# Routing attention and a hard-swish feed-forward block on one core: the first batch's second product in seven half products, and the weight sums in one row

## The chip, the cores and the metric

One core of a Trainium2 chip runs the whole program. The metric is the device time of one execution in microseconds (us). The engines are named as the profile names them: PE (TensorE matmul), PEld (its weight load), DVE (VectorE), ACT (ScalarE), POOL (GpSimd) and SP (SyncE, which issues the DMAs here).

## The reference

Four batches of 768 tokens go through an attention with 8 heads of 64, in which a query sees only the keys of its own cluster, and then through a feed-forward block with 512 inputs, 2048 hidden units and 512 outputs:

```
q_assign = argmax(q_n . c_n); k_assign = argmax(k_n . c_n)          # 16 clusters for each head
scores   = where(q_assign == k_assign, (q @ k^T) / 8, -1e9)
x        = softmax(scores) @ v                                      # (4, 8, 768, 64) -> (3072, 512)
h        = x @ w_in                                                 # (3072, 2048)
g        = h * clip(h + 3, 0, 6) / 6
out      = g @ w_out                                                # (3072, 512)
```

The inputs q, k, v and centroids are float32; the two weight matrices arrive as float64.

## The kernel before, in words

The program is one list of instructions in an order written out by hand, with no scheduler inside it. A loop runs over n = 0, 2, 4, ... and each turn of it, called "step n" here, handles attention units n and n+1. A unit is one block of 128 keys against half (384) of the queries, for a pair of heads. Twelve units make a pair of heads, 48 a batch, 192 all. A step emits, in this order:

- `scores` of units n and n+1 (L354 into the PSUM tile ps, then the exponential on ACT, L366, then an add into acc on POOL, L370 or L373, from the second unit of a half on);
- `attn_v` of the two units before (L383, into pv);
- every third step `divide` (pd by TensorE from the sum acc, L404; its reciprocal on VectorE, L408; and the product into xT, L409). It comes at steps 8, 14, 20 and so on, among them 56, 62, 68, 74, 80, 86, 92 and 98;
- preparation of the next pair: in the steps with n mod 12 equal to 0 and 2 two `turn`s each (pqk, L278, copied to xf by ACT, L280), at 4 `cluster_scores` (pcs, L291), at 6 `route` (pr by TensorE, L302, and then seven VectorE operations up to one_hot, L306 to L322), at 8 and 10 `route_turn` (po, L334);
- some feed-forward items from the list `fill`, alternating with the preparation (first an item, then a preparation part, and so on);
- in 32 chosen steps, the last of them step 94, `decode_weights`: one chunk of a weight matrix is turned from float64 into float32 by five VectorE operations (L217, L221, L224, L228, L231) and two on ACT (L208, L211). Its raw data were loaded by an SP DMA one decoding step earlier.

A batch's feed-forward items can begin when its last xT is there. The first batch's are added at step 50; the function `items_by(n)` says how many items must have been emitted by step n. DECODED is 96, the step after the last decode, and END is 104.

Two kinds of items exist before the change. `ffn_items`, for the first batch only, is the plain form: an up item is four matmuls of 384 columns into ph (L440), followed by the gate (ACT L427, VectorE L428); a down item is four matmuls of 512 columns into py (L457), and four of them make a row block of the output. For a half batch these are 16 ups and 12 downs. `fast_items`, for the other three batches, works on blocks of 256 tokens (m = 0, 1, 2). An up item is eight matmuls of 256 columns (L504), a gate 512 wide, and after every second one four VectorE sums of the gated blocks (L516, the S sums). Then seven down items, each one half product: eight matmuls of 256 columns (L522) into the banks X and Y, with five adds (L529 to L557) and two copies, in place of the eight half products of a plain 2x2 block product. In the profile every float32 matmul has two records, so that an up item of eight matmuls shows as 16.

Seven half products need sums of the weight blocks: `weight_sums(i)`, i = 0 to 7, makes T1, T2, T4 and T3 in halves, each one VectorE subtraction of 128x1024 (L493). T3 overwrites one quarter of w_out itself. Before the change the eight are emitted one a step, in steps 96 to 110, at the end of the step.

PSUM: ps has two double banks, pv one, and the rest is two pools: `psum_m` with two banks, which ph, py, X and Y take from, and `psum_t` with one. The helper `scratch` serves pqk, pcs, pr, po and pd; up to step 96 it takes two of three from psum_m and the third from psum_t, and from step 96 on (`st["early"] = False`) all from psum_t.

Of the kernel before, what the change touches and what calls it, by code (L numbers as in the profile page):

```python
# [8 lines left out]
F32 = mybir.dt.float32  # L9
# [9 lines left out]
P = 128  # L19
NCH = S // P  # L20
NC2 = 2 * NCH
HALF = S // 2
NHC = NCH // 2
# [93 lines left out]
def fast_path(ctx, tc, ok, q, k, v, centroids, moe_w_in, moe_w_out, out):  # L117
# [310 lines left out]
        nc.vector.scalar_tensor_tensor(out=g, in0=g, scalar=1.0, in1=h, op0=ALU.min, op1=ALU.mult)  # L428


    def ffn_items(b):
        slots = g_sb.rearrange("p k i c -> p (k i c)")

        def up(hf, f):
            def item():
                xT = st["xT", b]
                ph = psum_m.tile([P, 512], F32, name="ph", tag="m")
                hh = ph[:, 0:HALF]
                for kt in range(NKT):
                    nc.tensor.matmul(  # L440
                        hh, lhsT=w_in_sb[:, kt, f * P : (f + 1) * P],
                        rhs=xT[:, kt, hf * HALF : (hf + 1) * HALF],
                        start=(kt == 0), stop=(kt == NKT - 1),
                    )
                at = (hf * NFT + f) % 18 * HALF
                st["g", f] = slots[:, at : at + HALF]
                gate(st["g", f], hh)

            return item

        def down(hf, i, part):
            def item():
                if part == 0:
                    st["y"] = psum_m.tile([P, DM], F32, name="py", tag="m")
                py = st["y"]
                for f in range(part * 4, part * 4 + 4):
                    nc.tensor.matmul(  # L457
                        py, lhsT=st["g", f][:, i * P : (i + 1) * P], rhs=w_out_sb[:, f],
                        start=(f == 0), stop=(f == NFT - 1),
                    )  # L460
                if part == 3:
                    y = yp.tile([P, DM], F32, name="y", tag=f"y{i % 2}")
                    nc.vector.tensor_copy(out=y, in_=py)
                    nc.sync.dma_start(out_v[b, hf * NHC + i], y)

            return item

        items = []
        for hf in range(2):
            items += [up(hf, f) for f in range(NFT)]  # L470
            items += [down(hf, i, part) for i in range(NHC) for part in range(4)]
        return items

# [15 lines left out]
        nc.vector.tensor_tensor(out=st[name][:, h], in0=a[:, h], in1=b[:, h], op=ALU.subtract)  # L493


    def fast_items(b):
        def up(m, i):
            def item():
                xT = st["xT", b]
                ph = psum_m.tile([P, 512], F32, name="ph", tag="m")  # L500
                for t in range(2):
                    f = t * HF + i
                    for kt in range(NKT):
                        nc.tensor.matmul(  # L504
                            ph[:, t * HC : (t + 1) * HC], lhsT=w_in_sb[:, kt, f * P : (f + 1) * P],
                            rhs=xT[:, kt, 2 * m * P : 2 * (m + 1) * P],
                            start=(kt == 0), stop=(kt == NKT - 1),
                        )
                gate(g_sb[:, 0:4, i], ph.rearrange("p (k c) -> p k c", k=4))
                if i % 2:  # L510
                    a11, a21, a12, a22, s1, s2, s4 = (g_sb[:, k, i - 1 : i + 1] for k in range(7))
                    for out_, in0, in1, op in (
                        (s1, a21, a22, ALU.add), (s2, s1, a11, ALU.subtract),
                        (a21, a11, a21, ALU.subtract), (s4, a12, s2, ALU.subtract),
                    ):
                        nc.vector.tensor_tensor(out=out_, in0=in0, in1=in1, op=op)  # L516

            return item

        def product(bank, half, kind, w, first, last, again):  # L520
            for i in range(HF):
                nc.tensor.matmul(  # L522
                    bank[:, half * HC : (half + 1) * HC], lhsT=g_sb[:, kind, i], rhs=w[:, i],
                    start=(first and i == 0), stop=(last and i == HF - 1),
                    skip_group_check=again,
                )

        def add(out_, in0, in1):
            nc.vector.tensor_tensor(out=out_, in0=in0, in1=in1, op=ALU.add)  # L529

        def down(m, part):
            def item():
                if part == 0:
                    st["X"] = psum_m.tile([P, DM], F32, name="X", tag="m")
                    st["y0"] = yp.tile([P, DM], F32, name="y0", tag="y0")
                elif part == 2:
                    st["Y"] = psum_m.tile([P, DM], F32, name="Y", tag="m")
                    st["y1"] = yp.tile([P, DM], F32, name="y1", tag="y1")
                kind, bank, half, w = (
                    (0, "X", 0, wb[0][0]), (5, "X", 1, st["T2"]),  # L540
                    (4, "Y", 0, st["T1"]), (1, "Y", 1, st["T3"]),
                    (2, "X", 0, wb[1][0]), (6, "Y", 0, wb[1][1]), (3, "Y", 1, st["T4"]),
                )[part]
                product(st[bank], half, kind, w, part in (0, 2), part in (1, 3, 4, 6), part > 3)
                y0, y1 = st["y0"], st.get("y1")
                if part == 1:
                    nc.scalar.copy(out=y0[:, HC:], in_=st["X"][:, HC:])
                    add(y0[:, HC:], y0[:, HC:], st["X"][:, 0:HC])
                elif part == 3:
                    add(y1[:, 0:HC], y0[:, HC:], st["Y"][:, HC:])  # L550
                    add(y1[:, HC:], y1[:, 0:HC], st["Y"][:, 0:HC])
                elif part == 4:
                    nc.scalar.copy(out=y0[:, 0:HC], in_=st["X"][:, 0:HC])
                elif part == 6:
                    add(y1[:, 0:HC], y0[:, HC:], st["Y"][:, HC:])
                    nc.sync.dma_start(out_v[b, 2 * m + 1], y1)
                    add(y0[:, HC:], y0[:, HC:], st["Y"][:, 0:HC])  # L557
                    nc.sync.dma_start(out_v[b, 2 * m], y0)

            return item  # L560

        items = []
        for m in range(NHC):
            items += [up(m, i) for i in range(HF)] + [down(m, part) for part in range(7)]
        return items
# [20 lines left out]
    per_batch = NKT * per_pair  # L586
    total = NPAIR * per_pair
    lag_v, lag_d = 2, 4
    up_half = NFT
    per_ffn = 2 * (NFT + NHC * 4)  # L590
    per_fast = NHC * (HF + 7)

# [8 lines left out]
    def items_by(n):  # L603

        if n <= DECODED:
            return max(n - READY, 0) * up_half // (DECODED - READY)
        if n <= END:
            return up_half + (n - DECODED) * (per_ffn - up_half) // (END - DECODED)
        return per_ffn + (n - END) * per_fast // per_batch

    st["early"] = True
    fill, later = [], []
# [2 lines left out]
    with tc.manual_schedule():  # L615
# [16 lines left out]
        for n in range(0, total + lag_d + 2, 2):  # L632
            g, r = divmod(n, per_pair)
            for i in (n, n + 1):
                if i < total:
                    scores(i)
            for i in (n - lag_v, n - lag_v + 1):
                if 0 <= i < total:
                    attn_v(i)
            for check in later:  # L640
                check()
            later = []
            m = n - lag_d + 1
            if m >= 0 and m % NCH == NCH - 1:
                later.append(divide(m))
            prep = prep_items(g + 1, r)
            if r == 4 and prep:
                prep.pop()()
            if n == DECODED:
                st["early"] = False  # L650
            if m >= 0 and m % per_batch == per_batch - 1:
                fill += (fast_items if m >= per_batch else ffn_items)(m // per_batch)
            if r == 6:
                load(g + 2, "q", "k")
                load(g + 1, "v")
            want = items_by(n + 2) - done if n < total else len(fill)
            want = min(want, len(fill))
            done += want
            for i in range(max(len(prep), want)):
                if i < want:  # L660
                    fill.pop(0)()
                if i < len(prep):
                    prep[i]()
            if n in slots:
                load_weights(slots.index(n) + 1)
                decode_weights(slots.index(n))
            if n >= DECODED and (n - DECODED) // 2 < 8:
                weight_sums((n - DECODED) // 2)
            if n >= total:
                for check in later:  # L670
                    check()
                later = []
# [381 lines left out]
```

## Time and profile before

| | us |
|---|---|
| median of 10 runs | 1108.46 (1107.1 to 1109.28) |
| the profiled execution: its time | 1108.44 |
| the profiled execution: its span, first to last instruction | 1106.6 |
| PE, DVE, ACT, POOL busy in the span | 1049.0, 466.9, 384.8, 301.3 |
| mean granted PE clock | 0.983 of full speed |

Times in the profile count from the start of the span. A row of a group gives line, engine, operation, output<-inputs, count, busy time in us and the mean of one in ns. Rows of the chain give a start and a length in us, and follow the work that ended last back to what released it. Step 48 begins at 138.0 us (its first exponential), step 96 at 304.9, and the matmuls of step 104's up item at 447.0.

### The profile page before, as it was taken

The numbers are of one execution on the slowest core, as the hardware profiler recorded it, in microseconds if no ns is written. First come the engines' busy times: TensorE is split into PE (matmuls) and PEld (weight loads), VectorE is DVE, ScalarE is ACT, GpSimd is POOL, SyncE is SP. The second block draws the span as 40 slices with busy tenths as digits, with TensorE's granted clock in tenths as the row PEclk, the third lists the DMA queues.
The fourth block names the chain that finished last, engine by engine and source line by source line (L and its number), as shares of the span: only waits on it lengthen the run. The fifth ranks groups of instructions, "written<-read, shape, count | busy, mean of one in ns | idle before, by whom it ended". The sixth has DMA issues, their size and how long they took to land.

```text
span 1106.6 us, 12777 instructions
## 1 busy us (share of the span) xinstructions
PE 1049.0 (95%) x5218; PEld 674.6 (61%) x5218; DVE 466.9 (42%) x654; ACT 384.8 (35%) x734; POOL 301.3 (27%) x187
## 2 busy tenths in 40 slices
PE   5988888999799999999999999999999999999996
PEld 3433334444344544676676777667676678888885
DVE  6799996688612220342240332333133141413131
ACT  4666665666411310332333332332333230101010
POOL 3666653554401100323222232322323320000000
PEclk8999998999899999999999999999999999999999
DMA  5333341342202000020110202001100000000000
GB/s 130 90 93 88 94 119 58 101 119 70 69 10 59 3 1 20 10 43 1 33 30 1 63 1 44 20 12 32 34 1 1 20 1 1 20 4 16 20 1 24
DMA packets 83541, 42.90 MB, mean 39 GB/s; under 512 B 76304, under 2 KB 76304, under 8 KB 83472
## 3 DMA queue, kind: packets, MB, share of 16 engines
q1 hardware_dynamic: 83328, 41.95, 14.7%
q8 instruction: 43, 0.70, 0.3%
q14 instruction: 26, 0.21, 0.1%
q10 hardware_dynamic: 144, 0.03, 0.0%
HBM read 35.68 MB, written 6.29 MB: 38 GB/s over the span
## 4 chain that ended last, share of the span: by engine, by line
PE 81%; DVE 16%; issue 1%; ACT 1%; POOL 0%; DVEq 0%; POOLq 0%
PE ph L504 23%; PE Y L522 11%; PE ps L354 11%; PE X L522 9%; PE pv L383 8%; PE py L457 7%; PE ph L440 6%; DVE rcp L408 3%; DVE wtop L221 2%; DVE one_hot L322 2%; DVE wtop L217 2%; PE pqk L278 2%; DVE wunit L228 1%; DVE xT L409 1%; PE pd L404 1%
## 5 line engine op out<-in xcount | busy, mean ns | idle before, releaser
L373 POOL TENSOR_TENSOR acc<-acc,ex 128x768 f32<-128x768 f32 x128 | 239.1, 1868 | 405.5 <-ACT ex L366 400.0
L504 PE MATMUL ph<-xT,w_in_sb 128*128 128x256 f32 x1152 | 259.6, 382 | 0.0
L504 PEld LDWEIGHTS ph<-xT,w_in_sb 128*128 128x128 f32 x1152 | 215.3, 190 | 46.2 <-issue 18.1
L366 ACT ACTIVATE ex<-ps 128x768 f32<-128x768 f32 x192 | 151.0, 806 | 150.8 <-PE ps L354 149.7
L428 DVE SCALAR_TENSOR_TENSOR g_sb<-g_sb,ph 128x512 f32<-128x512 f32 (+1 forms) x104 | 67.1, 645 | 282.6 <-ACT g_sb L427 282.6
L354 PE MATMUL ps<-xf 64*128 64x384 f32 x768 | 172.8, 529 | 5.2 <-ACT ex L366 5.2
L427 ACT ACTIVATE g_sb<-ph,half_c 128x512 f32<-128x512 f32 (+1 forms) x104 | 68.1, 655 | 313.9 <-PE ph L504 249.6
L383 PE MATMUL pv<-ex,vt 128*64 128x384 f32 x768 | 146.4, 503 | 0.0
L370 POOL TENSOR_TENSOR acc<-ex 128x768 f32<-128x768 f32 x32 | 59.4, 1857 | 200.3 <-ACT ex L366 200.3
L408 DVE RECIPROCAL rcp<-pd 128x384 f32<-128x384 f32 x32 | 81.7, 2553 | 62.0 <-PE pd L404 62.0
L354 PEld LDWEIGHTS ps<-xf 64*128 64x128 f32 x768 | 65.8, 193 | 53.2 <-issue 34.6
L383 PEld LDWEIGHTS pv<-ex,vt 128*64 128x64 f32 x768 | 47.1, 138 | 82.9 <-issue 79.5
L440 PE MATMUL ph<-xT,w_in_sb 128*128 128x384 f32 x256 | 87.3, 493 | 2.0 <-DVE g_sb L428 2.0
L457 PE MATMUL py<-w_out_sb,g_sb 128*128 128x512 f32 x192 | 84.0, 594 | 0.0
L440 PEld LDWEIGHTS ph<-xT,w_in_sb 128*128 128x128 f32 x256 | 47.2, 190 | 41.5 <-issue 4.8
L529 DVE TENSOR_TENSOR y<-y,Y 128x256 f32<-128x256 f32 x36 | 15.1, 420 | 125.4 <-PE Y L522 124.8
L522 PE MATMUL Y<-w_out_sb,g_sb 128*128 128x256 f32 x288 | 66.1, 383 | 0.0
L354 PE MATMUL ps<-xm 64*128 64x384 bf16 x384 | 65.2, 334 | 0.7 <-ACT xm L338 0.7
L522 PE MATMUL Y<-T,g_sb 128*128 128x256 f32 x288 | 65.3, 380 | 0.0
L522 PE MATMUL X<-w_out_sb,g_sb 128*128 128x256 f32 x288 | 65.3, 380 | 0.0
L457 PEld LDWEIGHTS py<-w_out_sb,g_sb 128*128 128x128 f32 x192 | 35.9, 190 | 44.2 <-issue 43.0
L522 PEld LDWEIGHTS Y<-w_out_sb,g_sb 128*128 128x128 f32 x288 | 53.9, 190 | 12.9 <-issue 6.0
(88 smaller groups left out, 854.8 us busy)
## 6 DMA issues: line engine op xcount, KB each, us to landing
raw<-in_moe_w_in_dram SPq DMA_DIRECT2D x16, 512.0 KB, 3.6
raw<-in_moe_w_out_dram SPq DMA_DIRECT2D x16, 512.0 KB, 3.6
qk<-in_q_dram SPq DMA_DIRECT2D x32, 192.0 KB, 3.8
qk<-in_k_dram SPq DMA_DIRECT2D x32, 192.0 KB, 4.3
vt<-in_v_dram SPq DMA_DIRECT2D x32, 192.0 KB, 4.2
out_dram<-y SPq DMA_DIRECT2D x24, 256.0 KB, 2.1
cen<-in_centroids_dram ACTq DMA_DIRECT2D x1, 32.0 KB, 1.7
```

Source lines behind the costliest of these rows:

```text
L354: nc.tensor.matmul(st["ps", n][:, t, 0:HALF], lhsT=x[r, NCH + j], rhs=x[r, hf * NHC : (hf + 1) * NHC], start=first, stop=not first,)
L366: nc.scalar.activation(out=ex, in_=sc, func=ACT.Exp, scale=SM_SCALE)
L370: nc.gpsimd.tensor_tensor(out=acc, in0=st["ex", n - 1], in1=ex, op=ALU.add)
L373: nc.gpsimd.tensor_tensor(out=acc, in0=acc, in1=ex, op=ALU.add)
L383: nc.tensor.matmul(pv[t * D : (t + 1) * D], lhsT=vt[:, j, t], rhs=ex[:, t], start=(j == 0), stop=(j == NCH - 1),)
L408: nc.vector.reciprocal(out=rcp, in_=pd)
L427: nc.scalar.activation(out=g, in_=h, func=ACT.Relu, bias=half_c, scale=1.0 / 6.0)
L428: nc.vector.scalar_tensor_tensor(out=g, in0=g, scalar=1.0, in1=h, op0=ALU.min, op1=ALU.mult)
L440: nc.tensor.matmul(hh, lhsT=w_in_sb[:, kt, f * P : (f + 1) * P], rhs=xT[:, kt, hf * HALF : (hf + 1) * HALF], start=(kt == 0), stop=(kt == ...
L457: nc.tensor.matmul(py, lhsT=st["g", f][:, i * P : (i + 1) * P], rhs=w_out_sb[:, f], start=(f == 0), stop=(f == NFT - 1),)
L504: nc.tensor.matmul(ph[:, t * HC : (t + 1) * HC], lhsT=w_in_sb[:, kt, f * P : (f + 1) * P], rhs=xT[:, kt, 2 * m * P : 2 * (m + 1) * P], sta ...
L522: nc.tensor.matmul(bank[:, half * HC : (half + 1) * HC], lhsT=g_sb[:, kind, i], rhs=w[:, i], start=(first and i == 0), stop=(last and i == ...
```

## The change

The first batch's feed-forward block uses the same items as the other three: `ffn_items` in its plain form is gone and `fast_items` takes its name. The first batch then has 45 items for 56: 24 ups and 21 downs. By step 96 eight of its up items are to be emitted, where there were 16 of the smaller ones. At step 96 one item is emitted where there were ten; at steps 98, 100 and 102 twelve each where there were ten. All eight weight sums are emitted at step 94, behind the last decode. Line numbers move: the up matmuls are L460, the S sums L472, the down matmuls L478, the adds L485, the weight sums L449.

```diff
-    def ffn_items(b):
-        slots = g_sb.rearrange("p k i c -> p (k i c)")
-        def up(hf, f):
...
-                for kt in range(NKT):
-                    nc.tensor.matmul(
-                        hh, lhsT=w_in_sb[:, kt, f * P : (f + 1) * P],
-                        rhs=xT[:, kt, hf * HALF : (hf + 1) * HALF],
...
-        def down(hf, i, part):
...
-                for f in range(part * 4, part * 4 + 4):
-                    nc.tensor.matmul(
-                        py, lhsT=st["g", f][:, i * P : (i + 1) * P], rhs=w_out_sb[:, f],
...
-    def fast_items(b):
+    def ffn_items(b):
...
-    up_half = NFT
-    per_ffn = 2 * (NFT + NHC * 4)
-    per_fast = NHC * (HF + 7)
+    up_first = NFT // 2
+    per_ffn = NHC * (NFT // 2 + 7)
...
         if n <= DECODED:
-            return max(n - READY, 0) * up_half // (DECODED - READY)
+            return max(n - READY, 0) * up_first // (DECODED - READY)
         if n <= END:
-            return up_half + (n - DECODED) * (per_ffn - up_half) // (END - DECODED)
-        return per_ffn + (n - END) * per_fast // per_batch
+
+            n, first = max(n - 2, DECODED), up_first + 1
+            return first + (n - DECODED) * (per_ffn - first) // (END - 2 - DECODED)
+        return per_ffn + (n - END) * per_ffn // per_batch
...
-                fill += (fast_items if m >= per_batch else ffn_items)(m // per_batch)
+                fill += ffn_items(m // per_batch)
...
                 decode_weights(slots.index(n))
-            if n >= DECODED and (n - DECODED) // 2 < 8:
-                weight_sums((n - DECODED) // 2)
+                if n == slots[-1]:
+                    for i in range(8):
+                        weight_sums(i)
```

More of the change, by code (lines that the diff above doesn't have):

```diff
@@ L428, in gate @@
         nc.vector.scalar_tensor_tensor(out=g, in0=g, scalar=1.0, in1=h, op0=ALU.min, op1=ALU.mult)
-    def ffn_items(b):
-        slots = g_sb.rearrange("p k i c -> p (k i c)")
-        def up(hf, f):
[L435 to L438, printed above, removed]
-                for kt in range(NKT):
-                    nc.tensor.matmul(
-                        hh, lhsT=w_in_sb[:, kt, f * P : (f + 1) * P],
-                        rhs=xT[:, kt, hf * HALF : (hf + 1) * HALF],
[L443 to L449, printed above, removed]
-        def down(hf, i, part):
[L452 to L455, printed above, removed]
-                for f in range(part * 4, part * 4 + 4):
-                    nc.tensor.matmul(
-                        py, lhsT=st["g", f][:, i * P : (i + 1) * P], rhs=w_out_sb[:, f],
[L459 to L472, printed above, removed]
     HF, HC = NFT // 2, DM // 2
```

## The prediction

> **What bounds the kernel now.** I read the page first. TensorE is busy for 95% of the span and carries 81% of the chain that ended last, so the program as a whole is bound by TensorE; but 16% of the chain is VectorE's, and that share isn't spread evenly.
>
> ```profile
> span 1106.6 us, 12777 instructions
> PE 1049.0 (95%) x5218; PEld 674.6 (61%) x5218; DVE 466.9 (42%) x654; ACT 384.8 (35%) x734; POOL 301.3 (27%) x187
> ...
> PE 81%; DVE 16%; issue 1%; ACT 1%; POOL 0%; DVEq 0%; POOLq 0%
> ```
>
> Then busy time by stage. The first row is steps 12 to 48, three pairs with decoding and no feed-forward work; the second is steps 48 to 96, four pairs with faster decoding and the first batch's first 16 up items; the third is steps 96 to 104, the block in which the rest of that batch is run off. Columns are start:end, length, and busy time of PE, PEld, DVE, ACT and POOL.
>
> ```profile
> 48.20:138.00 89.80, 76.41 (x491) 33.80 (x489) 87.56 (x75) 60.99 (x127) 57.34 (x30) 0.98 0.37 93
> 138.00:304.90 166.90, 147.70 (x784) 70.76 (x782) 129.32 (x157) 100.34 (x219) 76.69 (x40) 0.94 0.34 89
> 304.90:447.00 142.10, 142.10 (x438) 68.17 (x434) 25.12 (x39) 21.66 (x38) 12.84 (x7) 1.00 0.07 20
> ```
>
> Stage one is VectorE's: busy 87.56 of 89.80 us. The block is TensorE's, without a gap. Stage two is mixed: TensorE has 19 us idle, and VectorE 38, of which only some 15 have GpSimd idle too (the two engines' rows laid over one another in the timeline). That matters because VectorE's rows are stretched when GpSimd runs its adds:
>
> ```profile
> L231 DVE TENSOR_TENSOR w_out_sb<-wtop,wunit x16: 683/692/2179, 173.2 to 305.8; 128x512 f32<-128x512 f32 x16
> L373 POOL TENSOR_TENSOR acc<-acc,ex x128: 1802/1816/2222, 23.5 to 905.9; 128x768 f32<-128x768 f32 x128
> L408 DVE RECIPROCAL rcp<-pd x32: 2543/2557/2559, 40.2 to 942.4; 128x384 f32<-128x384 f32 x32
> L493 DVE TENSOR_TENSOR T<-w_out_sb,T x4: 1215/1218/1220, 399.3 to 464.3; 128x1024 f32<-128x1024 f32 x4
> ```
>
> Minimum, median and maximum in ns: a decode's last operation takes 0.69 us alone and 2.18 with an add in its way; the reciprocal is never stretched. Last, the chain in order of time (start, length) at the join of stage two and the block:
>
> ```profile
> 285.42 3.15 DVE one_hot L322 x2
> ...
> 291.55 2.48 DVE rcp L408
> ...
> 294.07 1.01 PE po L334 x8
> 295.08 3.02 PE ps L354 x12
> ...
> 302.54 1.82 PE ps L354 x12
> 304.36 1.44 PE pv L383 x8
> 305.80 3.63 PE py L457 x8
> ```
>
> TensorE waits 5.6 us for the reciprocal of step 92 (its bank holds what po wants), and the first scores after that gap take 3.02 us instead of 1.82. The last decode ends at 306.50; nothing on TensorE hangs on VectorE again for a long time.
>
> **The matmuls.** Durations here are from the chain, so overlap is already taken out. Before, the first batch has 32 up items and 24 down items: 16 ups in stage two at 2.79 us, 44.6; in the block 125.6 us of feed-forward work (16 ups at 2.59, since 64 records take 20.64 and 20.84; 24 downs at 3.43). After, it has 24 up items and 21 down items, each 16 records of 128x256. Other batches show these: 3.65 us each when alone in a step, and in the undisturbed tail 27.63 for 8 ups and 24.2 for 7 downs, so 3.45 each. Eight ups in stage two: 29.2. The other 37 in the block: 127.8 plus some 0.8 for restarts, 128.6. So TensorE is relieved of 12.4 us in all; but stage two loses 15.4 and the block gains 3.0. The question is whether stage two gets shorter when TensorE has less to do in it.
>
> **VectorE in stage two.** Removed: 16 gates of 0.55 us. Added: 8 gates of 0.69 (512 wide) and four batches of four S sums at 0.42. Net: -8.8 + 5.5 + 6.7, 3.4 us more. To bound the stage from below I build a pair from stage one, where VectorE never rests: 29.9 us for a pair, plus two more decodes at 3.05, plus two gates at 0.72 and one set of S sums at 1.75, is 39.2; four make 156.8, call it 157. The same sum for the kernel before (four gates at 0.58, no S sums) gives 38.3 a pair, 153.3; it took 166.9. So 13.6 us are waits, mostly of VectorE for a gate's matmuls. With eight gates for sixteen and TensorE less loaded I keep a little over a third of these, 5 us (TensorE is also spared the 5.6 us wait at step 92: in the changed program's order the bank that po takes there is the one that the up item of step 90 has left). That puts the last decode at 306.5 - 166.9 + 157 + 5, about 301.5. Bounds: no waits left, 296.8; all 13.6 kept, 310.4.
>
> **The eight weight sums.** Each is 1.22 us. Before, they are spread over steps 96 to 110, one a step, under a TensorE that is full: they cost nothing. After, all eight stand on VectorE directly behind the last decode, and behind them the reciprocal of step 98. Who waits for it: from step 96 on every scratch tile is taken from the one bank of psum_t; pd of step 98 fills it, and the third turn (pqk) of the same step needs it, standing on TensorE behind a single down item, with ten more items of the block behind it. Part 1 of the first down also needs T2, but that is complete after four sums. So TensorE may go on when 8 x 1.25 (with the gap between instructions) + 2.6 = 12.6 us have passed since the last decode, plus what GpSimd's adds put between. Step 97's add and step 98's two may fall there. None of L493's rows was stretched (none ran beside much GpSimd work): 0; if each add holds a sum up for its whole length, 3 x 1.82 = 5.5. I take one and a half, 2.7, after L231, the nearest row by operands (two inputs in SBUF), less the add that may fall on the unstretched reciprocal.
>
> A rule of the Trainium skill speaks here against the change: SBUF — State Buffer, section "Who interferes with whom", says that a VectorE instruction with two SBUF inputs contends with a GpSimd instruction that reads SBUF, and that the later one is blocked outright until the other has finished. L231's 2179 ns against 692 agrees. By it all three adds count, and the total below would be 1116.6; by L493's row alone it would be 1111.1.
>
> **The sum.** The reciprocal of step 98 ends at 301.5 + 12.6 + 2.7 = 316.8. From there to the first matmul of step 104's up item, 447.02 before, TensorE has the rest of the block: 35 items at 3.45, 120.9; restarts, 0.6; and the attention work of steps 98 to 104, 12.5 (scores 1.82 and pv 1.44 three times, pd 0.65, pcs 0.78, pr 0.49, two turns). Together 134.0. The same count for before (16 ups, 13 downs from 348.4) gives 98.6, and it took 98.6. So that point comes at 450.8, 3.8 later. TensorE reaches the third turn some 6 us early and stands still; by the rows after the 5.61 us gap (3.02 for 1.82, and po 1.01 for eight where four take 0.22 elsewhere) restarting costs about 1.6. Everything later is the same program with the same TensorE work, and the weight sums that vanish from steps 98 to 110 were off the path. The profiled execution took 1108.44 (span 1106.6 and 1.8 around it; the median is 1108.46): 1108.44 + 5.4 = 1113.8.
>
> ScalarE's gates and copies have slack (22 us busy in the block of 142), SyncE's queue gets no new transfer, and y's stores are as in the other batches, where they stop nobody: these I put at nothing. If a y buffer were late, a store's landing of 2.1 us would be the price.
>
> **Rivals.** *Faster: stage two follows TensorE.* If VectorE's waits vanish altogether (last decode at 296.8) and the sums meet no add, the reciprocal ends at 309.4 and step 104's matmul comes at 443.4: 3.6 early, 1104.8. For it: TensorE has 10 of its 16 early ups on the chain. Against it: VectorE already carries 3.4 us more, and stage one shows that it has nothing left to give at 98%. The full 12.4 (1096) would need the third turn not to wait, and it stands behind the sums in program order.
>
> *No change.* Last decode at 299, one add in the way, a wait too short for a slow restart: 313.4, and 447.4 against 447.02; 1108.8. Break-even is a reciprocal that ends at 313.0.
>
> *Slower still: stage two doesn't shrink.* One mechanism: GpSimd's adds, which before ran while VectorE waited for gates, now meet decodes. Then nearly all of the 13.6 us return as stretched decodes, the last decode ends at 308, and two adds hit the sums: 324.2, step 104 at 458.2, 11.2 late, with the restart 12.8: 1121. It decides from the point where the last decode ends later than before, 306.5. Against it: fewer ups must free something.
>
> That the change wouldn't do what it says I rule out: the built order has 168 products of 256 columns for 96 of 512, and the sums in one row.
>
> **Chances.** Forecast 0.48, slower still 0.17, no change 0.14, faster 0.21. About 0.2% (2.2 us) can be told from nothing; the ten runs spread over 2.2. Slower by more: 0.65; within: 0.14; faster by more: 0.21. The range runs from the faster rival's 1104.8, a little below, to 1120, near the slower rival.
>
> **What would show it.** Right: eight L449 rows in one row behind the last L231, near 301 to 316; then L408; a TensorE gap of 4 to 8 us before a pqk, released by that L408, followed by slow matmuls; stage two (steps 48 to 96) shorter by less than 10 us. The first batch's matmuls should add up to 12 us less. Wrong: no gap before that pqk, or L449 rows ending before 308; then stage two was TensorE's after all and the time falls below 1106.

## The result, and the profile after

| | before | after |
|---|---|---|
| median, us | 1108.83 (28 runs) | 1115.58 (8 runs) |
| after to before | | 1.0063, 95% interval 1.0054 to 1.0071 |
| the profiled execution: time, span, us | 1108.44, 1106.6 | 1114.18, 1112.3 |

The change makes the kernel slower by 0.63%, 6.8 us between the medians; the two profiled executions are 5.7 apart. The forecast was 1113.8. The page of the changed kernel, lines as shown for the kernel before:

```profile
span 1112.3 us, 13383 instructions
PE 1041.2 (94%) x5490; PEld 728.0 (65%) x5490; DVE 503.2 (45%) x703; ACT 385.4 (35%) x732; POOL 303.1 (27%) x187
...
PE 76%; DVE 20%; issue 2%; ACT 1%; POOL 0%; DVEq 0%; POOLq 0%; ACTq 0%
```

TensorE has 8 us less to do and the program takes 6 longer: five points of the chain have gone from TensorE to VectorE and to issue. By stage (busy time of PE, PEld, DVE, ACT, POOL, then granted clock and DMA), from step 12, from step 48, and from step 96 to step 104's first up matmul:

```profile
48.20:138.00 89.80, 76.30 (x491) 33.83 (x489) 87.53 (x76) 61.09 (x127) 57.35 (x30) 0.98 0.36 93
137.70:297.80 160.10, 134.12 (x782) 71.16 (x780) 139.67 (x162) 96.97 (x209) 77.30 (x40) 0.94 0.35 93
297.80:452.90 155.10, 148.15 (x710) 121.10 (x706) 55.62 (x88) 25.68 (x45) 14.34 (x7) 0.98 0.07 18
```

Stage one is unchanged. Stage two takes 160.1 us for 166.9: 6.8 shorter, where TensorE lost 15.4 of work by the count; VectorE is busier in it than before in less time (139.67 of 160.1 for 129.32 of 166.9). Its waits for a gate's first half on ScalarE, before and after (total us, times, longest):

```profile
DVE g_sb L428 <- ACT g_sb L427: 31.7, 8, 9.1
DVE g_sb L428 <- ACT g_sb L427: 12.2, 5, 4.2
```

VectorE is spared 19.5 us of these waits, and still the stage is only 6.8 shorter: it is busy for 10.4 us more, with 3.4 us more of operations by the count. GpSimd's adds, which had run during the waits, now stretch its rows: the two engines run at the same time for 69.0 us of the stage, where it was 56.6 (the rows of the two laid over one another).

The block takes 13.0 more (155.1 for 142.1), and TensorE, which filled every microsecond of it before, now has 7 idle. The chain there, start and length:

```profile
302.07 0.70 DVE w_out_sb L231
...
302.80 10.14 DVE T L449 x6
312.93 2.27 DVE w_out_sb L449 x2
315.20 2.48 DVE rcp L408
...
317.73 0.90 PE pqk L278 x3
318.63 4.64 PE Y L478 x16
...
323.60 3.46 PE Y L478 x16
```

The last decode ends at 302.76, eight sums follow without a pause, then the reciprocal of step 98, and at 317.73 the third turn, for which TensorE had stood still since 311.35. The three matmuls of the turn take 0.90 us where the next three take 0.33, and the down item behind it 4.64 where the next takes 3.46: 1.75 us of slow restart. The sums' own rows (minimum, median, maximum in ns):

```profile
L449 DVE TENSOR_TENSOR T<-w_out_sb,T x4: 1209/2022/2837, 305.1 to 311.7; 128x1024 f32<-128x1024 f32 x4
L449 DVE TENSOR_TENSOR w_out_sb<-w_out_sb x2: 1209/1210/1210, 312.9 to 314.0; 128x1024 f32<-128x1024 f32 x2
```

And from the timeline of GpSimd in that stretch (start, length), the two adds of step 98 that ran among them:

```profile
305.86 4.86 POOL L373 TENSOR_TENSOR acc<-acc,ex 128x768 f32<-128x768 f32 x2 [4.37 <-ACT ex L366]
```

Their own rows, in ns:

```profile
L373 POOL TENSOR_TENSOR acc<-acc,ex x2: 2102/2388/2675, 305.9 to 308.0; 128x768 f32<-128x768 f32 x2
```

Eight sums took 12.4 us. Undisturbed ones start 1.13 us after one another here (the last two took 2.27 on the chain), so eight would take 9.2: the two adds put 3.2 between. They did so in two places: two of the sums took 2.84 and 2.83 us, the other six 1.21 to 1.23. The first of these two ended 1.09 us after the first add, the second add 1.67 us after that sum, and the second stretched sum 1.09 us after the second add; alone a sum takes 1.21 and an add 1.82. So the two engines took turns, one waiting until the other was all but done.

### The profile page after: what moved, and what is told of

It reads as the page before. It is cut to its first block, busy times and chain, and to the rows that moved or that the text cites. A ratio compares the mean times of both kernels' runs of the same rounds, so it can differ in the third digit from the quotient of the medians.

```text
span 1112.3 us, 13383 instructions
## 1 busy us (share of the span) xinstructions
PE 1041.2 (94%) x5490; PEld 728.0 (65%) x5490; DVE 503.2 (45%) x703; ACT 385.4 (35%) x732; POOL 303.1 (27%) x187
## 4 chain that ended last, share of the span: by engine, by line
PE 76%; DVE 20%; issue 2%; ACT 1%; POOL 0%; DVEq 0%; POOLq 0%; ACTq 0%
PE ph L460 29%; PE Y L478 15%; PE X L478 11%; PE ps L354 10%; PE pv L383 7%; DVE rcp L408 3%; DVE wtop L221 2%; DVE wunit L228 2%; DVE one_hot L322 2%; DVE wtop L217 2%; DVE xT L409 1%; PE pqk L278 1%; DVE wunit L224 1%; PE pd L404 1%; DVE T L449 1%
## 5 line engine op out<-in xcount | busy, mean ns | idle before, releaser
L460 PE MATMUL ph<-xT,w_in_sb 128*128 128x256 f32 x1536 | 345.7, 382 | 1.5 <-DVE rcp L408 1.5
L460 PEld LDWEIGHTS ph<-xT,w_in_sb 128*128 128x128 f32 x1536 | 287.4, 190 | 63.1 <-issue 21.7
L428 DVE SCALAR_TENSOR_TENSOR g_sb<-g_sb,ph 128x512 f32<-128x512 f32 x96 | 65.9, 686 | 268.0 <-ACT g_sb L427 268.0
L427 ACT ACTIVATE g_sb<-ph,half_c 128x512 f32<-128x512 f32 x96 | 66.0, 688 | 320.3 <-PE ph L460 320.3
L485 DVE TENSOR_TENSOR y<-y,Y 128x256 f32<-128x256 f32 x48 | 20.2, 420 | 174.6 <-PE Y L478 173.9
L478 PE MATMUL Y<-T,g_sb 128*128 128x256 f32 x384 | 88.3, 383 | 0.0
L478 PE MATMUL Y<-w_out_sb,g_sb 128*128 128x256 f32 x384 | 87.8, 382 | 0.0
L478 PE MATMUL X<-w_out_sb,g_sb 128*128 128x256 f32 x384 | 87.1, 380 | 0.0
L478 PEld LDWEIGHTS Y<-w_out_sb,g_sb 128*128 128x128 f32 x384 | 72.1, 190 | 15.4 <-issue 6.0
L478 PEld LDWEIGHTS Y<-T,g_sb 128*128 128x128 f32 x384 | 73.2, 193 | 9.7
L478 PEld LDWEIGHTS X<-w_out_sb,g_sb 128*128 128x128 f32 x384 | 72.4, 190 | 10.2 <-ACT ex L366 0.6
L472 DVE TENSOR_TENSOR g_sb<-g_sb 128x256 f32<-128x256 f32 x192 | 76.2, 438 | 3.3
L338 ACT CAST xm<-po 128x512 bf16<-128x512 f32 x48 | 27.5, 582 | 59.0 <-PE po L334 59.0
```

Source lines behind the costliest of these rows:

```text
L338: nc.scalar.copy(out=xm[:, part * 4 : part * 4 + 4], in_=po)
L427: nc.scalar.activation(out=g, in_=h, func=ACT.Relu, bias=half_c, scale=1.0 / 6.0)
L460: nc.tensor.matmul(ph[:, t * HC : (t + 1) * HC], lhsT=w_in_sb[:, kt, f * P : (f + 1) * P], rhs=xT[:, kt, 2 * m * P : 2 * (m + 1) * P], sta ...
L478: nc.tensor.matmul(bank[:, half * HC : (half + 1) * HC], lhsT=g_sb[:, kind, i], rhs=w[:, i], start=(first and i == 0), stop=(last and i == ...
```

## The experiments

My theory: the gap and the restart are the price of the reciprocal's place behind the sums, and stage two doesn't shrink with TensorE's work because VectorE, together with GpSimd, sets it. The rivals: the matmuls of the first batch cost more than counted, or stage two is TensorE's. Ratios are to the kernel before on the same chip, with 95% intervals.

### Four sums behind the reciprocal

```diff
-                    for i in range(8):
+                    for i in range(4):
                         weight_sums(i)
...
                 later.append(divide(m))
+                if n == DECODED + 2:
+                    for i in range(4, 8):
+                        weight_sums(i)
```

> The changed kernel, with four of the eight weight sums (T4, T3) emitted behind the reciprocal of step 98 instead of ahead of it. Theory (TensorE's 6.4 us gap before the third turn of step 98 is the reciprocal's place behind eight sums): the reciprocal ends 5 us or a little more earlier, near 312, about when TensorE gets there (311.4 in the changed kernel); the gap falls below 1.5 us, the slow restart (1.7 us) goes, and the time is 1107.5 to 1110 where the changed kernel has 1115.6. Part 3 of the first down may wait for T3 for under 1 us. Rival (the loss lies in the matmuls of the first batch, or in the stage before, and the gap only shows it): the reciprocal comes earlier, but the time stays within 2 us of 1115.6.

Measured: 1106.49 us, ratio 0.9980 (0.9969 to 0.9992); 9.2 us below the changed kernel by the ratios. Its chain at the same place:

```profile
302.97 6.25 DVE T L449 x4
309.22 2.48 DVE rcp L408
...
311.75 0.55 PE pqk L278 x3
312.29 3.46 PE Y L478 x16
```

The reciprocal ends 6.0 us earlier, at 311.70, 0.2 after TensorE gets there (311.51), and the down item behind the turn runs at full speed. The gap and the restart made 8.1 us; the rest of the 9.2 is within the two intervals. The median is 1 us below the range I gave. The theory holds; the matmuls of the first batch are the same here, and not the cause.

### The turns of step 98 behind its items

```diff
+            if n == DECODED + 2:
+                for i in range(want):
+                    fill.pop(0)()
+                for part in prep:
+                    part()
+                want, prep = 0, []
             for i in range(max(len(prep), want)):
```

> The changed kernel, with the two turns of step 98 emitted behind that step's twelve feed-forward items instead of between them. Nothing is added or removed. Theory: the sums and the reciprocal stay as late as they are (317 to 318), but nothing on TensorE waits for them within 40 us: no gap before the third turn, no slow restart, 8 us less: 1106.5 to 1109. Rival (matmuls or the stage before): within 2 us of 1115.6. Second rival (the next wait takes over: T3 for part 3 of the first down, or the sum y0 on VectorE for part 4): a gap of 3 us or more at one of these and a time of 1111 or above.

Measured: 1107.93 us, ratio 0.9993 (0.9983 to 1.0004). All sums stay ahead of the reciprocal:

```profile
316.42 2.48 DVE rcp L408
...
319.55 0.34 DVE y L485
...
319.94 3.72 PE X L478 x16
```

The reciprocal ends at 318.90, as late as in the changed kernel, and nobody waits for it. The next on the list does: the fifth half product needs VectorE's sum into y0, which stands behind that reciprocal, and TensorE waits 0.47 us for it. So the late reciprocal alone costs nothing; what costs is a matmul behind which the rest of the block is queued. The second rival was right in its place and wrong in its size.

### The sums in one row, with the plain first batch

The kernel before, with T1, T2 and T4 in one row behind the last decode and T3 where it was.

```diff
                 decode_weights(slots.index(n))
+                if n == slots[-1]:
+                    for i in range(6):
+                        weight_sums(i)
-            if n >= DECODED and (n - DECODED) // 2 < 8:
+            if n in (DECODED + 12, DECODED + 14):
                 weight_sums((n - DECODED) // 2)
```

> The kernel before, with the plain first batch, but with six of its eight weight sums (T1, T2, T4) in one row behind the last decode; the last two stay at steps 108 and 110, since T3 overwrites a part of w_out that the plain items still need. Theory: TensorE has ten items in step 96, 34 us, ahead of the reciprocal of step 98, so the row costs nothing: within 0.2% of the kernel before. Rival (a row of sums costs by itself, by holding up GpSimd's adds or the gates): 3 to 7 us more than the kernel before.

Measured: 1108.81 us, ratio 1.0002 (0.9994 to 1.0011): nothing. One sum was even held up by step 97's add here:

```profile
L493 DVE TENSOR_TENSOR T<-w_out_sb x2: 1212/1988/2764, 306.7 to 309.4; 128x1024 f32<-128x1024 f32 x2
```

The row of sums is free as long as step 96 has ten items to put before the third turn. It is the pair of the two edits, a row of sums and one item in step 96, that costs. (One item in step 96 with the sums spread as before was not run; the run with four sums behind the reciprocal, which waits 0.2 us, comes nearest.)

### More S sums

The changed kernel, with s1, s2 and s4 of the first block made twice: twelve VectorE operations of 0.42 us more, 5.1 us.

```diff
+                    for out_, in0, in1, op in (
+                        (s1, a21, a22, ALU.add), (s2, s1, a11, ALU.subtract), (s4, a12, s2, ALU.subtract),
+                    ) if b == m == 0 else ():
+                        nc.vector.tensor_tensor(out=out_, in0=in0, in1=in1, op=op)
                     for out_, in0, in1, op in (
```

> The changed kernel, with three of the four S sums of the first block of the first batch made twice: twelve more VectorE operations of 0.42 us in steps 62 to 94, 5.1 us. Theory (the stage up to the last decode is VectorE's and GpSimd's, not TensorE's): the last decode and with it the reciprocal of step 98 end 3 to 5 us later, the gap before the third turn grows by as much less what the up items are delayed, and the time is 1117.5 to 1121. Rival (TensorE sets that stage): the sums go into VectorE's idle time, 1115 to 1116.5.

Measured: 1129.76 us, ratio 1.0196 (1.0180 to 1.0213): 14.7 us above the changed kernel by the ratios, for 5.1 us of work. The rival is out, and my size is too small by a factor of three. Stage two, from the windows, in the same columns as above:

```profile
137.80:311.30 173.50, 138.22 (x784) 72.85 (x782) 147.68 (x171) 97.15 (x211) 76.59 (x40) 0.91 0.32 86
```

And its chain at the third turn of step 98, start and length:

```profile
332.55 0.90 PE pqk L278 x3
333.45 5.85 PE Y L482 x16
```

The stage is 13.4 us longer, and that is nearly all of the loss. The gap before the third turn did not grow, as I had said it would: it is 5.0 us for 6.4, since TensorE now waits 2.4 us for T2 ahead of it. The restart behind the turn is slower than in the changed kernel (5.85 us for 4.64). In stage two VectorE is busy 8.0 more, the sums and some 3 us of stretching, and idle 5.4 more (25.8 for 20.4), nearly all of it in waits for gates (17.3 for 12.2). TensorE is idle 9.3 us more (35.3 for 26.0), and its granted clock falls from 0.94 to 0.91. So the two wait for each other more than before; in what order one wait brings on the next is my reading, and no run shows it.

### No early up items

```diff
-    up_first = NFT // 2
+    up_first = 0
```

> The changed kernel with none of the first batch's up items before step 96 (one in step 96, then 14, 15 and 15 items): the stage from step 48 to step 96 has no gate, no S sum and no up item. Theory (VectorE and GpSimd set the stage): a pair is 29.9 us plus two decodes at 3.05, 36.0, and the stage 144 to 150 where the changed kernel has 160.1; eight items at 3.45 go to the block, 27.6, so the time is 11 to 18 us above the changed kernel's 1115.6, at 1127 to 1133. Rival (TensorE sets the stage, so it shrinks by the 29.2 us of its up items): 131 us, and 1112 to 1117 in all.

Measured: 1124.06 us, ratio 1.0149 (1.0126 to 1.0173), 9.5 above the changed kernel by the ratios, a little under the range I gave. Stage two:

```profile
138.30:281.40 143.10, 112.50 (x670) 50.49 (x665) 137.96 (x143) 92.12 (x203) 76.62 (x40) 0.89 0.39 104
```

With no feed-forward work at all it still takes 143.1 us, 12 more than the rival allows; the pair built from stage one said 144. VectorE is busy for 96% of it, and TensorE is idle for 31 us. Taking feed-forward work away can't bring stage two below this.

### Half the early items in the plain kernel

```diff
-    up_half = NFT
+    up_half = NFT // 2
```

> The kernel before (plain first batch) with 8 of its 16 half-batch up items before step 96 instead of 16. That takes 22.3 us of matmuls and 4.4 us of gates out of the stage from step 48 to 96, adds no S sums, and adds 8 items at 2.59, 20.7 us, to the block. Theory: the stage is VectorE's, a pair 29.9 + 6.1 + 1.2 = 37.2, four 148.8 plus some waits: 150 to 156 where the kernel before has 166.9, and 1112 to 1119 in all. Rival (TensorE sets the stage): 144.6, and 1107 or below. Set beside the changed kernel (160.1, the same number of gates, more matmul time, and the S sums) the stage also tells what the S sums cost: 5 to 10 us by the run with more of them.

Measured: 1111.70 us, ratio 1.0038 (1.0026 to 1.0051). Stage two:

```profile
137.80:286.10 148.30, 125.25 (x707) 58.49 (x708) 131.43 (x149) 96.05 (x210) 77.45 (x40) 0.93 0.39 100
```

148.3 us, just under the range I gave, as the time is, and at the 148.8 that the pair makes with no waits. But the waits are not gone: VectorE is idle for 16.9 us, 7.6 of them for a gate. Its rows are less stretched instead (busy 131.43, where stage one's pair has it busy nearly throughout), so the agreement with the pair is luck. The stage gives back 18.6 us for 22.3 of matmuls, which is more than the changed kernel's did (6.8 for 15.4). It would fit a TensorE-set one within 4 us, so this run doesn't separate the theories. Nor does it price the S sums: the changed kernel's stage, 11.8 us longer, has 6.9 us more of matmuls too.

### The S sums out of stage two

The run with four sums behind the reciprocal, and the first block's S sums taken out of its up items: s1 and s2 behind T1 and T2, the other two behind the reciprocal.

```diff
-                if i % 2:
+                if i % 2 and (b or m):
...
+        def first_sums(late):
+            a11, a21, a12, a22, s1, s2, s4 = (g_sb[:, k] for k in range(7))
...
                         weight_sums(i)
+                    st["first_sums"](0)
...
+                    st["first_sums"](1)
-                    for i in range(4, 8):
+                    for i in (6, 7, 4, 5):
```

> The run with T4 and T3 behind the reciprocal, and on top the S sums of the first block taken out of the stage before the last decode: s1 and s2 are made behind T1 and T2, 1024 wide (1.2 us each), the other two behind the reciprocal of step 98. Theory (VectorE sets that stage, and each S sum in it costs its length or more): the stage from step 48 to 96 shrinks from 160 to 150 to 155, the first down item that needs s2 and T2 then waits some 4 us for them, and the time is 2 to 6 us below that run's 1106.5: 1101 to 1104.5. Rival (TensorE sets the stage; the sums only filled gaps): the stage stays at 159 to 161, and the time is 1106 to 1110.

Measured: 1103.74 us, ratio 0.9958 (0.9940 to 0.9976): faster than both kernels, and below the run with four sums behind the reciprocal (0.9980), though the ends of the two intervals overlap slightly. Stage two, from the windows:

```profile
138.20:289.60 151.40, 131.09 (x771) 69.81 (x772) 133.07 (x149) 96.73 (x210) 76.86 (x40) 0.95 0.37 98
```

The chain where stage two meets the block, start and length:

```profile
291.40 6.12 DVE T L449 x4
297.52 1.15 DVE g_sb L482
298.67 0.02 issue
298.69 2.72 DVE g_sb L482
...
301.46 3.72 PE X L488 x16
```

Stage two is 151.4, against 160.4 with the S sums in it: 9.0 us for 6.7 us of operations, the last set of which stands at the very end. TensorE waits 2.0 us for s2 (I expected 4). But the profiled execution is one of this kernel's shortest, 1099.22 with a median of 1103.74, and from the first exponential of step 104 to the end all kernels here take the same (661.6 to 662.8 us), so it is stage two or what lies before it that is short in it. The gain is read from the ratio, 2.4 us; the block is 1.7 longer than in the run without the move, so by an estimate from these the S sums cost a typical execution some 4 us. Between 4 and 9, their price stays open.

## Why the prediction was right

**The matmuls.** Foretold: 12.4 us less in all, stage two 15.4 less and the block 3.0 more. By TensorE's rows the up items of stage two take 29.3 us for 44.6, 15.3 less; the block's feed-forward items take 129.8 for 124.5, 5.3 more, of which 1.2 is slow restart. So 11.2 us less without the restart. The prediction's 125.6 for the block before doesn't follow from its own items (16 at 2.59 and 24 at 3.43 make 123.8); the sum doesn't use it.

**The last decode.** Foretold 301.5, measured 302.76, within its bounds of 296.8 and 310.4 (as added up there, 296.6 and 310.2). The number is right, but the terms behind it are not. The prediction took 13.6 us for VectorE's waits in stage two before, and kept 5. In the trace it waits 31.7 us for gates there, 12.2 in the changed kernel, and of the 19.5 saved some 7 come back as stretched rows (10.4 us busier for 3.4 of operations). A wait of VectorE that GpSimd's adds can use is not all lost: before, neither engine ran for only 17.5 us (the prediction says some 15). That 5 us fitted is luck. Stage two itself ended 7.0 us earlier, not 5; but in its last step the S sums and an operation stretched by an add (L228, 2.18 us) now stand ahead of the end of the last decode, which came only 3.7 earlier. What the S sums cost isn't settled. The pair built from stage one was right for a stage without feed-forward work: 144 against 143.1.

**The reciprocal behind the sums.** Foretold: end at 316.8, 15.3 us after the last decode (12.6 and 2.7 for adds); measured 317.68, 14.9 after. Two sizes were off and cancelled: eight sums alone take 9.2 us and not 10.0, since there is no gap between them but an overlap, and the adds cost 3.2 and not 2.7. Each of the adds that met a sum cost 1.62 of its 1.82 us, and two did: step 97's fell into the last decode, step 98's two into the sums, none on the reciprocal. The Trainium skill's rule (SBUF — State Buffer, "Who interferes with whom") is borne out by L449's 2837 ns beside its 1209, and L493's even rows before were even because at most 0.3 us of an add ran beside any of them. The full hold for three adds, 5.5 us, was too much in the count of adds and nearly right for each.

**The gap.** Foretold: 4 to 8 us before a turn, released by that reciprocal, with 1.6 of restart. Measured: 6.38 and 1.75. Two runs that remove it in different ways, and touch neither the matmuls nor the number of sums, take 9.2 and 7.8 us off.

**The sum.** Step 104's up item at 450.8 plus the restart, 452.4; it came at 452.93, 5.9 later than before. The medians lie 6.8 us apart, 0.9 more than that, since the profiled run after is one of its faster ones (1114.18, runs from 1114.13 to 1117.01).

**A step that failed.** I had TensorE spared the 5.6 us wait before po of step 92, since po takes another bank. It no longer waits for the reciprocal, but it waits 4.79 us for one_hot, which VectorE makes ahead of that reciprocal. Here a wait that was taken from TensorE came back at another result of the busier engine.

**The rivals.** "Faster" needed stage two to follow TensorE; a stage with no TensorE feed-forward work at all takes 143.1. "Slower still" foresaw adds meeting decodes. They do: VectorE is busy 139.67 us in stage two for 129.32, but the waits saved were larger. In the experiment with more S sums stage two is longer than before the change, as that rival had it: 14.7 us of time for 5.1 of sums.

## What to carry to other kernels

Before moving work in front of an instruction on an in-order engine, find who waits for that instruction and what is queued behind the waiter: six of the sums cost nothing with ten items in one step ahead of the waiting turn, and all eight held TensorE up for 0.47 us with thirteen items ahead of it, but for 6.4 us and a slow restart with two. Taking matmuls out of a stage that another engine sets gains little, and adding small operations to that other engine can cost more than they last: nearly three times as much in one run here. An edit that is harmless alone is priced again at the place where it meets the others.

## What the runs showed of the hardware that I had not expected

A VectorE sum with both inputs in SBUF and a GpSimd add did not slow each other, they took turns: two adds of 1.82 us lengthened the row of eight sums by 3.2 us, and took 4.86 us together themselves. The reciprocal, which reads PSUM, was not touched: in the run with four sums behind it an add ran beside it for 1.75 us, and it took 2545 ns where the median is 2557. So the same add costs VectorE nothing or nearly its whole length, by what it meets. And small VectorE operations in a stage where VectorE and TensorE wait for each other in turn cost far more than they last: 5.1 us of S sums made stage two 13.4 us longer, of which 5.1 are the sums, some 3 stretched VectorE rows and 5.4 new waits, with TensorE's granted clock down from 0.94 to 0.91. Which part of these waits comes from the clock and which from the order was not separated.
